# A recurrent transformer's backward chain: ScalarE's LayerNorm steps placed behind a copy, memory rows turned by TensorE, the first segment's rest rows picked by matmuls

## The chip, the cores and the metric

The kernel runs on one core of a Trainium2 chip. A core has TensorE (PE in the profile, its weight loads PEld), VectorE (DVE), ScalarE (ACT), GpSimd (POOL) and SyncE (SP); the last two also issue most of this kernel's DMAs, each engine working through its own list in order. The metric is device microseconds for one execution, as the median over runs.

## The reference

The forward is a LayerNorm, a recurrent attention over segments of 32 rows with 8 memory rows carried from one segment to the next, a second LayerNorm and a gated feed-forward layer (FFN). The kernel must return the output and the gradients of x, of the first memory and of the seven weights.

```
def _A_ref(x, mem0, Wq, Wk, Wv, Wo, seg_len):        # H=16 heads, Dh=256, M=8, D=448
    ...
    for s in range(n_seg):                            # 64 segments of 32 rows
        xs = x[:, s * seg_len:(s + 1) * seg_len, :].copy()
        h = jnp.concatenate([mem, xs], axis=1)
        q = jnp.einsum('btd,dhe->bhte', h, Wq)        # k and v alike
        ...
        scores = jnp.where(mask[None, None], scores, -1000000000.0)
        p = _softmax(scores, axis=-1)
        o = jnp.einsum('bhqk,bhke->bhqe', p, v)
        o = jnp.einsum('bhte,hed->btd', o, Wo)
        mem = o[:, :M, :].copy()
        outs.append(o[:, M:, :])
    return jnp.concatenate(outs, axis=1)
def _B_ref(x, w_gate, w_up, w_down):                  # F=1792
    return _silu(x @ w_gate) * (x @ w_up) @ w_down
h = x + _A_ref(_layernorm(x, axis=-1), A_mem0, A_Wq, A_Wk, A_Wv, A_Wo, A_seg_len)
h2 = h + _B_ref(_layernorm(h, axis=-1), B_w_gate, B_w_up, B_w_down)
# returned: h2 and the vector-Jacobian product with grad_out, x and weights in bf16
```

## The kernel before

The program has four stages: a forward chain over 64 segments, the FFN forward and backward by groups of two tiles of 128 rows, a backward chain over the segments from s = 63 down to 0, and a tail that forms the weight gradients from what the chain has stored. All loops are unrolled; a scheduler sets each engine's order from priorities and a model of the times. The block `k.prio.crit()` gives its work the highest priority. `tc.issue_after(ins)` holds what the block traces on the engine of `ins`, and on that engine alone, behind `ins` in the order; other engines' work in the block is free.

A tile t of 128 rows is four segments; r = s mod 4 counts down from 3 to 0, jm = s mod 16. In each segment TensorE forms the gradient by the output weights (L1180, evacuated to `dO_own`), turns it (L1190), multiplies for dV from the memory rows (`value_rest`, L1306, which reads `dOr` and the turned P rows `P4r`) and from the segment's own rows (`value_own`, L1312), and forms dP (L1429). VectorE makes dS from dP, from the loaded P (`P_sb`) and from its block-diagonal copy `P_bd`, which GpSimd writes (L1225). TensorE turns dS (L1475), and VectorE and ScalarE copy one half each (L75 and L76, the lines of the helper `k.evac`). The heads for dK and dQ follow (L1289), their rows are evacuated (`heads` and `first_rows`), and the rows are multiplied by the turned weights (L1324, and L1344 for the memory rows of a whole tile). The sum is taken over four partition groups (`summed`, L1330, from two ScalarE copies L1515), copied by VectorE (L1531) and turned (L1534) into the memory gradient that the next segment needs. L1531 is thus one instruction per segment, close to its end.

The LayerNorm backward of a tile runs two tiles later, inside the segments: `rest_sums_saved` stores the memory rows' sums to DXN at r = 3 (L1368), `norm_load` loads DXN, XN and DH at r = 2 (L1356 to L1359), `norm_first` is traced at the end of r = 2 and `norm_second` at the end of r = 1. Both are called in a block that holds their VectorE steps behind the last VectorE copy of `first_rows("q")`, `cast["v"]`. Their ScalarE activations are L1373 and L1384. The tile `x` of these steps appears in the profile as om; `om2`, the same buffer, also takes the memory rows' products at r = 0 (L1470).

Every 16 segments (jm = 0) the memory gradients gathered in `dmr` are turned to rows: four DMA transposes on SyncE (L1551) write `dhx`, and `memory_rows` stores it by four GpSimd DMAs (L381) to DC0 and DC1. The tile `dhx` is also the target of `prep_tile`'s DMA transpose at r = 3 (L1170) and, as `rO`, of evacuations at r = 2 and 1. The loads for the next segment on SyncE are `load_rest` (L1201, from RO), `load_p` (L1209), `load_v` (L1213) and `load_qk` (L1221); on GpSimd half of `load_p` (L1210) and P_sb (L1223).

The first segment, s = 63, is special: its memory rows' gradients are formed just ahead (b = 0, 1), stored to RO and loaded again by `load_rest(NSEG - 1)`, and its `value_rest` is placed after the scores instead of ahead of the turns:

```
            with tc.issue_after(last_d.ins):
                if s == NSEG - 1:
                    value_rest(pV)
                value_own(pV, 0 if s == NSEG - 1 else 4, 8)
```

Of the kernel before, what the change touches and what calls it, by code (L numbers as in the profile page):

```python
# [10 lines left out]
BF16 = mybir.dt.bfloat16  # L11
ALU = mybir.AluOpType
ACT = mybir.ActivationFunctionType
AX = mybir.AxisListType

P = 128
# [1116 lines left out]
def backward_chain(k: _K):  # L1133
    nc, tc = k.nc, k.tc
    S, D, M, H, Dh, HD = k.S, k.D, k.M, k.H, k.Dh, k.HD
    SEG, L, NSEG, NT, KC, DP, MC, DC = k.SEG, k.L, k.NSEG, k.NT, k.KC, k.DP, k.MC, k.DC
    ident, dr, sel = k.ident, k.dr, k.sel
    smal = k._small
    W, A, B = k.W, k.A, k.B
    OUT1, OUT2 = k.aps["out"][1][0], k.aps["out"][2][0]  # L1140
    NWIN = 8
    DQ = D // 4
# [7 lines left out]
    dmr = A(48, 4, 16, M)  # L1150
# [5 lines left out]
    do_roll = A(57.3125, 4, NWIN, L)  # L1156
    dhx = A(59.8125, 4, P)
    dOr = A(62.0625, 5, P)
# [5 lines left out]
    ot = k.identf[:, 0:DQ // 2].bitcast(BF16)  # L1164
# [22 lines left out]
    def grads_turned(bank, src, dst, b, eng="v"):  # L1187
        pt = bank[:].bitcast(BF16)
        for i in range(4):
            last = nc.tensor.transpose(pt[:, i * P:(i + 1) * P], src[:, i * P:(i + 1) * P], ident[:, :])  # L1190
        return last, k.evac(dst.rearrange("p (x c) n -> p x c n", x=2)[:, :, 8 * b:8 * b + 8, :],
                            pt[:, 0:512].rearrange("p (c x n) -> p x c n", x=2, n=32), eng)

    def rest_saved(t, b, src):
        nc.gpsimd.dma_start(out=dr["RO"][t][:, 512 * b:512 * b + 512], in_=src)

    def load_rest(s):
        t, r = divmod(s, 4)
        src = dr["RO"][t].rearrange("(q r k) n -> r q k n", q=4, k=M)
        for w, a, m, n in ((0, 0, 0, 3), (1, 0, 3, 3), (0, 3, 6, 2)):  # L1200
            nc.sync.dma_start(out=dOr[32 * w:32 * w + 32, a:a + n].rearrange("p m e -> p (m e)"), in_=src[r][:, :, P * m:P * (m + n)])  # L1201
# [49 lines left out]
    for c in range(4):  # L1251
        d0 = DQ * c
        while d0 < DQ * (c + 1):
            n = min(DQ * (c + 1), (d0 // P + 1) * P) - d0
# [13 lines left out]
    rO = dhx.rearrange("p c n -> p (c n)")  # L1268
# [3 lines left out]
    with k.prio.crit():  # L1272
        for b in range(2):
            pr, src = k.bank(b), (rO, A(46, 512))[b]
# [1 line left out]
            k.evac(src, pr[:], "vs"[b])  # L1276
            grads_turned(k.bank(2 + b), src, R4_b[(NT - 1) % 2], b, "vs"[b])
            rest_saved(NT - 1, b, src)
    load_rest(NSEG - 1)

    def c12(ps, b):
        n = min(12, 32 - 12 * b)
# [14 lines left out]
    def v_out(ps, m):  # L1297
        return v_bank(ps, m // 3)[2].rearrange("p (x m g n) -> p x m g n", x=2, g=2, n=L)[:, :, m % 3]

    def p_rows(rhs, m):  # L1300
        return rhs[:, :, m // 2].rearrange("p (x g) n -> p x g n", x=2)

    def value_rest(ps):
        for m in (0, 3, 1, 4, 2, 5, 6, 7):
            w, a = divmod(m, 3) if m < 6 else (0, m - 3)
            last = nc.tensor.matmul(v_out(ps, m), lhsT=dOr[32 * w:32 * w + 32, a, :], rhs=p_rows(P4r[32 * w:32 * w + 32], m),  # L1306
                                    start=m in (0, 3, 6), stop=False, skip_group_check=True)
        return last

    def value_own(ps, m0, m1):  # L1310
        for m in range(m0, m1):
            last = nc.tensor.matmul(v_out(ps, m), lhsT=dO_own[:, m * P:(m + 1) * P], rhs=p_rows(P4, m),  # L1312
                                    start=False, stop=True, skip_group_check=True)
        return last

    def v_rows(ps, b):
        m0, n, bank = v_bank(ps, b)
        return slice(2 * m0, 2 * m0 + 2 * n), bank.rearrange("p (x c n) -> p x c n", x=2, n=L)

    def rows_in(ps, lhs, WT, js, start=False, stop=False):  # L1320
        js = list(js)
        for i, j in enumerate(js):
            q = i % 4
            last = nc.tensor.matmul(ps[32 * q:32 * q + 32, 0:D], lhsT=lhs(j), rhs=WT[:, cj(j), :],  # L1324
                                    start=(start and i < 4), stop=(stop and i >= len(js) - 4), skip_group_check=True)
        return last
# [9 lines left out]
    def rest_parts(n):  # L1336
        last = None
        for _ in range(min(n, len(parts))):
            last = parts.pop(0)()
        return last  # L1340
# [26 lines left out]
        for q in range(4):  # L1367
            nc.gpsimd.dma_start(out=dst[q][:, 0:M], in_=pxs[32 * q:32 * q + 32])  # L1368

    def norm_first(t):  # L1370
        x, rstd, junk = norm[t][0], k.rstd1[:, t:t + 1], prod_t
        m1, m2 = [smal.tile([P, 1], FP32, name=f"lnb_m{i}") for i in (1, 2)]
        nc.scalar.activation(out=x[:], in_=x[:], func=ACT.Copy, accum_out=m1[:])  # L1373
        nc.vector.tensor_tensor_reduce(out=junk[:, 0:D], in0=x[:], in1=xn_t, scale=1.0, scalar=0.0,
                                       op0=ALU.mult, op1=ALU.add, accum_out=m2[:])
        m1s, m2s = [smal.tile([P, 1], FP32, name=f"lnb_m{i}s") for i in (1, 2)]
        nc.vector.tensor_scalar(out=m1s[:], in0=m1[:], scalar1=-1.0 / D, scalar2=rstd, op0=ALU.mult, op1=ALU.mult)
        nc.vector.tensor_scalar(out=m2s[:], in0=m2[:], scalar1=-1.0 / D, scalar2=None, op0=ALU.mult)
        nc.vector.scalar_tensor_tensor(out=x[:], in0=xn_t, scalar=m2s[:], in1=x[:], op0=ALU.mult, op1=ALU.add)
        norm[t][1] = m1s  # L1380

    def norm_second(t):
        x, m1s = norm.pop(t)
        nc.scalar.activation(out=x[:], in_=x[:], func=ACT.Identity, scale=k.rstd1[:, t:t + 1], bias=m1s[:])  # L1384
        for c0 in (0, 224):
            nc.vector.tensor_tensor(out=xn_t[:, c0:c0 + 224], in0=x[:, c0:c0 + 224], in1=dh_h[c0 // 224], op=ALU.add)
        nc.gpsimd.dma_start(out=OUT1[t * P:(t + 1) * P, :], in_=xn_t)

    V_FILL = {3: 16, 2: 16, 1: 16, 0: 3 * MC}
    for s in range(NSEG - 1, -1, -1):  # L1390
        t, r = divmod(s, 4)
        jm = s % 16
        sl = s % NWIN
# [12 lines left out]
        with k.prio.crit():  # L1406
# [6 lines left out]
            pool_op = nc.gpsimd.tensor_copy(out=doT[:, :, 0:M], in_=R4_b[t % 2][:, :, r * M:(r + 1) * M])  # L1413
# [1 line left out]
                with tc.issue_after(pool_op.ins):  # L1415
                    (rest_sums_saved if r == 3 else norm_load)(t + 2)
            pV = [k.bank(2 + b) for b in range(3)]
            if s < NSEG - 1:
                value_rest(pV)
            grads_turned(k.bank(0), dO_own[:, 0:512], doT[:, :, M:L], 0)  # L1420
            if s < NSEG - 1:
                value_own(pV, 0, 4)
            last_t, turned_v = grads_turned(k.bank(1), dO_own[:, 512:], doT[:, :, M:L], 1)

            def score_mm(hg):
# [13 lines left out]
            with tc.issue_after(last_t.ins):  # L1439
                last_d = score_mm([(1, 1), (5, 1)] + [(h, g) for h in (2, 3, 6, 7) for g in range(2)])  # L1440
            with tc.issue_after(last_d.ins):
                if s == NSEG - 1:
                    value_rest(pV)
                value_own(pV, 0 if s == NSEG - 1 else 4, 8)
            if s == 0:
                k.tl.grads(0)
                k.tl.outs(4, 7, 0, 6)
            for b in range(3):
                js, v = v_rows(pV, b)
# [10 lines left out]
            for b in range(3):  # L1460
                js, v = v_rows(pV, b)
# [11 lines left out]
            for h in range(8):  # L1473
                for g in range(2):
                    last_t = nc.tensor.matmul(pT[g][64 * g:64 * g + L, h * L:(h + 1) * L], lhsT=dS_bd[:, h, g, :],  # L1475
                                              rhs=ident[:, 64 * g:64 * g + L], start=True, stop=True, skip_group_check=True)
# [32 lines left out]
            last_r = rows_in(pH, lambda j: blk["q"][:, j, r * SEG:(r + 1) * SEG], WqT_sb, range(MC), stop=True)  # L1509
            cast = first_rows("q")  # L1510
# [7 lines left out]
            with tc.issue_after(last_r.ins):  # L1518
                if rest:
                    last_r = grads_by_col(rest_lhs, pR, 2 - r, 0, 2)  # L1520
                elif parts:
                    last_r = rest_parts(12)
            pq = k.bank(2)
            with tc.issue_after(last_r.ins):
                last_r = summed(pq, om)
            with tc.issue_after(last_r.ins):
                if rest:
                    grads_by_col(rest_lhs, pR, 2 - r, 2, 4)
                elif parts:
                    rest_parts(4)  # L1530
            nc.vector.tensor_copy(out=ot, in_=pq[:, 0:DQ])  # L1531
            if s > 0:
                pm = k.bank(3)[:].bitcast(BF16)
# [2 lines left out]
                                      in_=pm[0:DQ, 0:P].rearrange("p (c n) -> p c n", n=32)[:, :, 24:32])  # L1536
            else:
                for q in range(4):
                    nc.sync.dma_start(out=OUT2[:, DQ * q:DQ * q + DQ], in_=ot[32 * q + 24:32 * q + 32, :])
            nc.scalar.copy(out=dxs, in_=pq[:, 0:DQ])  # L1540
            if rest:
                k.evac(rO, pR[:], "s")
            if r in (2, 1) and t + 2 < NT:
                with tc.issue_after(cast["v"].ins):
                    (norm_first if r == 2 else norm_second)(t + 2)
        pool_op = nc.gpsimd.tensor_copy(out=dmr[0:DQ, :, jm, :], in_=do_roll[0:DQ, :, sl, SEG:L])
        stores("start", s, pool_op.ins)
        if jm == 0:
            rows = dhx.rearrange("p c n -> p (c n)")
            for c in range(4):  # L1550
                nc.sync.dma_start_transpose(out=rows[:, DQ * c:DQ * c + DQ], in_=dmr[0:DQ, c].rearrange("p s m -> p (s m)"))  # L1551
            k.tl.memory_rows(s // 16, rows)
        if s % 4 == 1 and 16 <= s < 48:
            with tc.issue_after(pool_op.ins):
# [20 lines left out]
    for t in (1, 0):  # L1575
        if t == 0:
            rest_parts(len(parts))
            nc.scalar.copy(out=om2[:], in_=pX[:, 0:D])
            rest_out()
        rest_sums_saved(t)  # L1580
        norm_load(t)
        norm_first(t)
        norm_second(t)
    assert not pending


# [243 lines left out]
```

## Time and profile before

| | |
|---|---|
| runs before, median (lowest, highest of 3) | 2954.59 us (2947.98, 2963.27) |
| profiled execution, its time | 2945.84 us |
| profiled execution, span of its instructions | 2943.8 us |
| mean granted TensorE clock | 0.980 |
| TensorE busy (matmul) | 2742.8 us, 93% |
| DVE, ACT, POOL busy | 1303.8, 1046.0, 930.3 us |
| backward chain, first to last L1531 | 1299.71 to 2258.21 us |

The page of the profile gives busy times, the span in slices, DMA queues, the chain of work that ended last, and the costliest groups of instructions. In timeline rows the columns are the start (us from the span's start), the duration in us, the engine, line, operation, the tiles written and read, the count, and in brackets the engine's idle time before the row with what ended it. "PEclk" and "granted clock" are the share of full speed that TensorE was given. A row of the waits gives who waited for whom, the total in us, how many times, and the longest. SPq and POOLq rows are DMA issues and other sequencer work.

### The profile page before, as it was taken

What the parts mean: (1) busy time and instruction counts of PE and PEld (TensorE: products, weight loads), DVE (VectorE), ACT (ScalarE), POOL (GpSimd) and SP (SyncE); (2) the same over time, 40 slices, a digit from 0 to 9 for tenths busy, and PEclk for the clock granted to TensorE, in tenths of its full rate; (3) what the DMA queues carried; (4) which work ended last, traced back from release to release, by engine and by line L of the source; (5) the groups of instructions that cost most, each with busy time, mean ns of one, the idle gap of its engine ahead of it and who ended that gap; (6) DMA issues with size and microseconds to landing.
All of it is one profiled execution on the core that took longest, in us unless ns stands there. A gap on an engine that the chain in (4) does not pass through costs nothing.

```text
span 2943.8 us, 97992 instructions
## 1 busy us (share of the span) xinstructions
PE 2742.8 (93%) x41631; PEld 1579.9 (54%) x41631; DVE 1303.8 (44%) x3351; ACT 1046.0 (36%) x2574; POOL 930.3 (32%) x2063
## 2 busy tenths in 40 slices
PE   4999999999999999979899998999998999999999
PEld 3555565566555556645555555555554444444444
DVE  4555555565555666734545554554543011111110
ACT  2555455454445444423333333333332010111210
POOL 1222232232232222424544445444453111112211
PEclk9999999999999999989999999999999999999999
DMA  7577777677678989976766667676677998969951
GB/s 256 154 191 192 194 193 195 187 196 200 196 192 238 273 216 215 244 229 161 173 162 174 167 161 181 168 178 167 161 169 201 351 261 183 171 190 229 190 158 53
DMA packets 784281, 572.06 MB, mean 194 GB/s; under 512 B 634748, under 2 KB 676100, under 8 KB 781284
## 3 DMA queue, kind: packets, MB, share of 16 engines
q1 hardware_dynamic: 719636, 407.84, 58.5%
q0 software_dynamic: 64208, 157.95, 17.1%
q8 instruction: 328, 5.37, 0.8%
q14 instruction: 109, 0.89, 0.1%
HBM read 181.64 MB, written 244.92 MB: 145 GB/s over the span
## 4 chain that ended last, share of the span: by engine, by line
PE 66%; DMA 10%; issue 9%; DVE 4%; POOL 4%; ACT 4%; SPq 1%; POOLq 0%; ACTq 0%; DVEq 0%
PE psf L1671 8%; PE bank L1324 6%; PE psf L590 6%; PE psf L725 5%; PE psf L988 4%; PE po L772 4%; PE bank L1180 4%; PE fx L1112 3%; PE fx L1671 3%; PE psf L614 2%; DMA arB<-P_all 2%; PE bank L1289 2%; PE bank L1344 2%; PE psf L506 1%; DMA DXN<-arA 1%
## 5 line engine op out<-in xcount | busy, mean ns | idle before, releaser
L75 DVE CAST arA<-psf 128x512 bf16<-128x512 f32 (+2 forms) x285 | 160.0, 562 | 491.9 <-PE psf L1671 249.9
L76 ACT CAST arA<-psf 128x512 bf16<-128x512 f32 (+3 forms) x379 | 190.0, 510 | 528.7 <-PE psf L1671 215.1
L1324 PE MATMUL bank<-arW,arA 128*32 128x448 bf16 x6144 | 327.6, 364 | 0.0
L76 ACT CAST arA<-bank 128x384 bf16<-128x384 f32 (+4 forms) x607 | 193.1, 376 | 113.7 <-PE bank L1312 98.6
L1671 PEld LDWEIGHTS <-arA 128*128 128x128 bf16 x1440 | 139.6, 99 | 162.4 <-issue 7.9
L1324 PEld LDWEIGHTS <-arA 128*32 128x32 bf16 x6144 | 158.2, 99 | 125.6 <-issue 13.1
L1671 PE MATMUL psf<-arW,arA 128*128 128x512 bf16 x882 | 224.6, 383 | 0.0
L725 PE MATMUL psf<-arW,arA 128*64 128x512 bf16 x1536 | 212.2, 382 | 0.0
L590 PE MATMUL psf<-arW,arA 128*32 128x512 bf16 x3072 | 189.8, 381 | 7.7 <-DVE arA L75 0.9
L988 PE MATMUL psf<-arW 128*128 128x256 bf16 (+1 forms) x1288 | 148.0, 276 | 5.6 <-DVE arA L75 4.3
L75 DVE CAST arA<-bank 128x384 bf16<-128x384 f32 (+4 forms) x385 | 130.4, 392 | 51.6 <-PE bank L1289 48.2
L1225 POOL COPY arB<-arB 40x320 bf16<-40x320 bf16 x128 | 68.0, 532 | 231.5 <-DMA arB<-P_all 193.1
L1748 POOL DMA_DIRECT2D out_dram<-arA x96 | 52.1, 544 | 263.6 <-DVE arA L75 236.9
L1210 POOL DMA_DIRECT2D arA<-P_all x256 | 128.0, 504 | 21.2 <-issue 20.4
L988 PEld LDWEIGHTS <-arW 128*128 128x128 bf16 (+1 forms) x1344 | 103.0, 97 | 56.9 <-issue 45.7
L1289 PE MATMUL bank<-arB,arW 128*128 128x80 bf16 x2048 | 96.2, 204 | 38.2 <-ACT arB L76 35.7
L1180 PE MATMUL bank<-arW,arA 112*32 112x512 bf16 x2048 | 129.0, 396 | 1.3 <-DVE arA L1535 1.3
L772 PE MATMUL po<-arW,arA 128*32 128x256 bf16 (+1 forms) x4096 | 126.9, 261 | 1.2 <-DVE arA L75 1.2
L590 PEld LDWEIGHTS <-arA 128*32 128x32 bf16 x3072 | 70.3, 96 | 105.1 <-issue 28.5
L1711 PE MATMUL psf<-arW 128*128 128x448 bf16 x525 | 114.5, 360 | 2.7 <-ACT arA L76 2.7
L772 PEld LDWEIGHTS <-arA 128*32 128x32 bf16 x4096 | 104.0, 96 | 8.5 <-DVE arA L75 1.5
L1289 PEld LDWEIGHTS <-arW 128*128 128x128 bf16 x2048 | 83.4, 101 | 45.3 <-issue 37.1
(311 smaller groups left out, 5050.5 us busy)
## 6 DMA issues: line engine op xcount, KB each, us to landing
arW<-T SPq DMA_DIRECT2D x256, 128.0 KB
X_o<-arA SPq DMA_DIRECT2D x37, 512.0 KB
T<-arA SPq DMA_DIRECT2D x64, 256.0 KB
X_v<-arA POOLq DMA_DIRECT2D x30, 512.0 KB, 4.6
X_k<-arA POOLq DMA_DIRECT2D x30, 512.0 KB, 3.9
X_q<-arA POOLq DMA_DIRECT2D x30, 512.0 KB, 4.7
out_dram<-arA POOLq DMA_DIRECT2D x84, 128.0 KB, 5.0
VG<-arA SPq DMA_DIRECT2D x64, 160.0 KB
```

The source lines that it names most:

```text
L75: return nc.vector.tensor_copy(out=out, in_=in_)
L76: return nc.scalar.copy(out=out, in_=in_)
L590: nc.tensor.matmul(banks[b][w][32 * q:32 * q + 32, :], lhsT=hT_roll[:, kc, sl, M:L], rhs=(Wq_sb, Wk_sb)[w][:, kc, col(q, b)], start=(b == ...
L725: nc.tensor.matmul(pV[b][64 * g:64 * g + 64, 0:512], lhsT=hT_flat[:, kc, sl * L:sl * L + 64], rhs=Wv_sb[:, kc, n * 512:(n + 1) * 512], sta ...
L772: last = nc.tensor.matmul(pO[32 * q:32 * q + 32, 0:w], lhsT=xblk[:, j, r * SEG:(r + 1) * SEG], rhs=Wo_sb[:, cj(j), 256 * dh:256 * dh + w], ...
L988: nc.tensor.matmul(ps[fp][:, f2 * 256:(f2 + 1) * 256], lhsT=Wt[lo:hi, kc, c * P:(c + 1) * P], rhs=xT[lo:hi, kc, :], start=(kc == 0 and f2 ...
L1180: last = nc.tensor.matmul(bank[32 * q:32 * q + 32, :], lhsT=lhs(c), rhs=WoT_sb[0:DQ, c, n0:n0 + 512], start=(c == 0), stop=(c == 3), skip_ ...
L1210: nc.gpsimd.dma_start(out=P4[32 * q:32 * q + 32, 2 * x + g], in_=pa[64 * g + M:64 * g + L, x])
L1289: last = nc.tensor.matmul(ps[b][:, i * 2 * L:(i + 1) * 2 * L], lhsT=lhs[:, at, :], rhs=rhs_bd[:, cl // 2, :, :].rearrange("p g n -> p (g n ...
L1324: last = nc.tensor.matmul(ps[32 * q:32 * q + 32, 0:D], lhsT=lhs(j), rhs=WT[:, cj(j), :], start=(start and i < 4), stop=(stop and i >= len( ...
L1671: k.last_mm = nc.tensor.matmul(pa[i][:, 0:w], lhsT=lhs_of(b)[:, i // 2 * P:(i // 2 + 1) * P], rhs=rhs_of(q, b, i % 2), start=(b == 0), sto ...
L1711: k.last_mm = nc.tensor.matmul(pa[i][:, 0:D], lhsT=lhs_of(b, i), rhs=rhs_of(b), start=(bi == 0), stop=(bi == m + 3))
```

## The change

Three edits in `backward_chain`. First, the activations of `norm_first` and `norm_second` are held on ScalarE behind `cast["s"]`, the ScalarE copy of `first_rows("q")` of the segment in which they are traced. Second, at jm = 0 the four DMA transposes are replaced by four TensorE transposes into bank 4, behind the last `summed` matmul, and a ScalarE copy into `dhx`; the GpSimd copy into `dmr` that feeds them is traced earlier and inside the high-priority block, in all segments. Third, `load_rest(NSEG - 1)` is replaced: GpSimd copies 32 columns of the identity into `one`, four matmuls with it pick the rows of r = 3 from the two halves still in SBUF, and two copies write `dOr`; `value_rest` and `value_own` of s = 63 stand where they do in all other segments.

```diff
-    load_rest(NSEG - 1)
+        one = ot[:, 0:32]
+        nc.gpsimd.tensor_copy(out=one.rearrange("p (q m) -> p q m", m=M), in_=ident[:, :].rearrange("p (q r m) -> p r q m", q=4, m=M)[:, 3])
+        half = A(46, 512)
+        pk = [k.bank(2), k.bank(3)]
+        for out, src in ((pk[0][0:32, 0:384], rO[:, 0:384]), (pk[0][32:64, 0:P], rO[:, 384:512]),
+                         (pk[0][32:64, P:384], half[:, 0:256]), (pk[1][0:32, 0:256], half[:, 256:512])):
+            nc.tensor.matmul(out, lhsT=one, rhs=src, start=True, stop=True, skip_group_check=True)
+        k.evac(dOr[0:64, 0:3].rearrange("p m e -> p (m e)"), pk[0][0:64, 0:384], "v")
+        k.evac(dOr[0:32, 3:5].rearrange("p m e -> p (m e)"), pk[1][0:32, 0:256], "s")
...
-    def norm_first(t):
+    def norm_first(t, after):
...
-        nc.scalar.activation(out=x[:], in_=x[:], func=ACT.Copy, accum_out=m1[:])
+        with tc.issue_after(after["s"].ins):
+            nc.scalar.activation(out=x[:], in_=x[:], func=ACT.Copy, accum_out=m1[:])
...
-    def norm_second(t):
+    def norm_second(t, after):
         x, m1s = norm.pop(t)
-        nc.scalar.activation(out=x[:], in_=x[:], func=ACT.Identity, scale=k.rstd1[:, t:t + 1], bias=m1s[:])
+        with tc.issue_after(after["s"].ins):
+            nc.scalar.activation(out=x[:], in_=x[:], func=ACT.Identity, scale=k.rstd1[:, t:t + 1], bias=m1s[:])
...
-            if s < NSEG - 1:
-                value_rest(pV)
+            value_rest(pV)
             grads_turned(k.bank(0), dO_own[:, 0:512], doT[:, :, M:L], 0)
-            if s < NSEG - 1:
-                value_own(pV, 0, 4)
+            value_own(pV, 0, 4)
...
             with tc.issue_after(last_d.ins):
-                if s == NSEG - 1:
-                    value_rest(pV)
-                value_own(pV, 0 if s == NSEG - 1 else 4, 8)
+                value_own(pV, 4, 8)
...
+            pool_op = nc.gpsimd.tensor_copy(out=dmr[0:DQ, :, jm, :], in_=do_roll[0:DQ, :, sl, SEG:L])
+            if jm == 0:
+                with tc.issue_after(last_r.ins):
+                    pr = k.bank(4)[:].bitcast(BF16)
+                    for c in range(4):
+                        nc.tensor.transpose(pr[:, DQ * c:DQ * c + DQ], dmr[0:DQ, c].rearrange("p s m -> p (s m)"), ident[0:DQ, 0:DQ])
             nc.vector.tensor_copy(out=ot, in_=pq[:, 0:DQ])
...
             nc.scalar.copy(out=dxs, in_=pq[:, 0:DQ])
+            if jm == 0:
+                rows = dhx.rearrange("p c n -> p (c n)")
+                k.evac(rows[:, 0:D], pr[:, 0:D], "s")
             if rest:
                 k.evac(rO, pR[:], "s")
             if r in (2, 1) and t + 2 < NT:
                 with tc.issue_after(cast["v"].ins):
-                    (norm_first if r == 2 else norm_second)(t + 2)
-        pool_op = nc.gpsimd.tensor_copy(out=dmr[0:DQ, :, jm, :], in_=do_roll[0:DQ, :, sl, SEG:L])
+                    (norm_first if r == 2 else norm_second)(t + 2, cast)
         stores("start", s, pool_op.ins)
         if jm == 0:
-            rows = dhx.rearrange("p c n -> p (c n)")
-            for c in range(4):
-                nc.sync.dma_start_transpose(out=rows[:, DQ * c:DQ * c + DQ], in_=dmr[0:DQ, c].rearrange("p s m -> p (s m)"))
             k.tl.memory_rows(s // 16, rows)
```

The two calls for the last tiles, after the loop, pass `cast` in the same way.

More of the change, by code (lines that the diff above doesn't have):

```diff
@@ L1581, in backward_chain @@
         norm_load(t)
-        norm_first(t)
-        norm_second(t)
+        norm_first(t, cast)
+        norm_second(t, cast)
     assert not pending
```

## The prediction

> **What bounds the kernel now.** I read the page first: TensorE is busy for 93% of the span, so only stretches in which it stands still, or runs below full clock, have time to give.
>
> ```profile
> span 2943.8 us, 97992 instructions
> PE 2742.8 (93%) x41631; PEld 1579.9 (54%) x41631; DVE 1303.8 (44%) x3351; ACT 1046.0 (36%) x2574; POOL 930.3 (32%) x2063
> ```
>
> The backward chain's length per segment can be read from the DVE rows of L1531, one at the end of each segment. The first comes at 1299.71, the last at 2258.21. With r = s mod 4, segments with r = 2 last 13.98 us, with r = 1 14.09, with r = 0 14.4 to 15.0 (medians or extremes of 15 or 16). With r = 3 they last 15.2 to 21.4, except s = 59, the only one without a LayerNorm step in flight: 13.84. So the loss sits in r = 3. The windows view, cut at the L1531 rows, for s = 51, 43, 35 and 59 (columns: window, length, busy PE, PEld, DVE, ACT, POOL, granted clock, DMA share, GB/s):
>
> ```profile
> 1456.87:1478.22 21.35, 16.03 (x275) 9.13 (x273) 7.13 (x18) 5.40 (x17) 10.86 (x22) 0.84 0.87 171
> 1583.70:1601.11 17.41, 15.31 (x275) 8.76 (x273) 7.04 (x18) 5.40 (x17) 11.39 (x25) 0.90 0.75 191
> 1704.62:1721.10 16.48, 13.62 (x275) 8.19 (x273) 7.04 (x19) 5.40 (x17) 9.60 (x19) 1.00 0.95 200
> 1341.32:1355.16 13.84, 13.62 (x275) 8.12 (x273) 6.95 (x19) 4.73 (x15) 7.75 (x19) 1.00 0.75 163
> ```
>
> The same matmuls (x275) take 13.62 us warm and up to 16.03 after a stall: a stall costs its idle time and then slow matmuls. Who stalls is in the timeline of s = 51:
>
> ```profile
> 1466.86 0.54 POOL L1356 DMA_DIRECT2D om<-DXN  x1 [3.90 <-DMA DXN<-arA]
> 1469.70 0.58 ACT L1373 ACTIVATE om<-om 128x448 f32<-128x448 f32 x1 [6.43 <-DMA om<-DXN]
> 1470.87 1.23 PE L1289 MATMUL bank<-arB,arW 128*128 128x80 bf16 x16 [5.14 <-ACT arB L76]
> 1472.02 5.06 PE L1324 MATMUL bank<-arW,arA 128*32 128x448 bf16 x64
> 1477.45 0.96 POOL L1225 COPY arB<-arB 40x320 bf16<-40x320 bf16 x2 [5.93 <-DMA arB<-P_all]
> ```
>
> ScalarE waits at norm_first's activation (L1373) for a load; behind it in ScalarE's order stands the second half of dS turned (L76), and TensorE's heads (L1289) wait for that. The waits of ScalarE between 1390 and 2245 us say how often, and the next two fences show the change's other two places: SyncE's transposes at s = 48 with the matmul that the loads behind them hold up, and the first segment.
>
> ```profile
> ACT om L1373 <- DMA om<-DXN: 54.9, 14, 6.5
> ```
>
> ```profile
> 1511.12 6.70 SPq L1551 DMA_TRANSPOSE arA<-arA  x4
> ...
> 1523.57 0.41 PE L1306 MATMUL bank<-arA 32*128 32x160 bf16 x2 [2.74 <-DMA arA<-P_all]
> ```
>
> ```profile
> 1286.85 0.58 PE L1306 MATMUL bank<-arA 32*128 32x160 bf16 x3 [11.48 <-DMA arA<-RO]
> 1280.00:1285.00 5.00, 0.00 (x0) 0.00 (x0) 0.00 (x0) 0.00 (x0) 0.00 (x0) 0.50 1.01 417
> 1290.00:1295.00 5.00, 5.00 (x61) 2.72 (x59) 0.81 (x2) 1.85 (x8) 2.18 (x5) 0.51 0.11 24
> ```
>
> **Part 1, the LayerNorm activations.** In the program text norm_first belongs to r = 2, but only its DVE steps are held there; L1373 ran 17 to 19 us ahead of them (1407.96 against 1424.95, 1469.70 against 1488.92), in r = 3, as soon as its load was thought to be there. Pinned behind the ScalarE copy of first_rows at the end of r = 2, it cannot stand in r = 3. The 14 segments with r = 3 that carry it (s = 55 to 3) sum to 261.8 us; 14 x 13.84 is 193.8; the excess is 68.0. Eleven of them (all but s = 47, 31, 15) have 199.3 - 152.2 = 47.1 of it. That is the gross gain.
>
> What is late next: POOL. It stops at L1356 until DXN has landed, and the loads of P for the next segment queue behind it. In the trace the copy L1225, which starts when P has landed, comes 13.6 to 21.6 us after the r = 3 segment began. The next segment reads P 5.04 us after its start, so with 13.84 long segments it is needed at 18.9. Three of the eleven rows are past it (20.6, 21.3, 21.6: 1.7 + 2.4 + 2.7 = 6.8 us). The ends are 0 and all fourteen as late as the worst, 38. The DMA engines were busy for 0.75 to 0.95 of the ordinary r = 3 segments, and the same transfers must now go through less time, so I take 12: nearer the three rows than the worst. Net 35.1.
>
> At its new place L1373 costs nothing by its cover: in r = 2 ScalarE is free from 1424.24 to 1426.65 and needs 0.58 + 0.19 us. DVE's L1374 to L1379 wait for it and end near 1426.7; L1531, queued behind them on DVE, ran at 1428.38. If that cover were gone it would cost up to the 1.7 us of these DVE steps each time. norm_second's L1384 (0.76 us) moves from the end of r = 2, where the copy L1515 stood behind it (TensorE idle 0.40 before L1330), to the end of r = 1, where ScalarE idles 2.68 us before L1515. The r = 2 segments without it last 13.74 (s = 58) against 13.98: 0.24 x 14 = 3.4 gained; ends 0 and 14 x 0.40 = 5.6.
>
> The slow matmuls: PE busy in these 14 segments sums to 211.4 us, 20.7 over 14 x 13.62; so 20.7 of the 68.0 are slower matmuls, at a granted clock of 0.83 to 0.92, and 47.3 idle time. The Trainium skill ("TensorE: Matmul & The Clock Gate", Part 1, What's actually happening) has the array drop to half clock only after an idle window of about 3.4 us. By that rule the 9.7 us of slow matmuls in s = 47, 43, 39, 27 and 19, whose longest gaps were 2.74, 1.97, 2.76, 3.18 and 3.07 us, would have another cause and stay. The trace speaks against it: the clock was 0.90 in s = 43 after a gap of 1.97 and 1.00 where nothing stalled, so the sum counts them as returned.
>
> **Part 2, memory rows.** At s = 48, 32, 16 and 0 the four DMA transposes go, 6.70 us of SyncE's queue at s = 48; the loads for s = 47 follow them at once. Four TensorE transposes come (four of L1190 take 0.40 us) and one ScalarE copy of 128x448 from PSUM (0.59 for 128x512); TensorE may pay 0.25 to 0.4 a time before L1534: 1.0 us in all. The copy is covered by ScalarE's 2 us gap after L1540; bank 4, which it empties, is next written by L1306's last three, some 2.7 us later. The three segments after, s = 47, 31 and 15, have 20.9 us of the excess, 10.9 of it TensorE idle at L1306. But the tile they leave, dhx, takes the next DMA transpose of a block on SyncE (L1170), which waits for POOL's four DC stores to land: it came 10.0 us into s = 47 against 3.2 in s = 51, and the loads for s = 46 stand behind it, ending 16.5 in. With 14 us segments that is late by 2 to 3 us. I return half: 10.5; ends 2 and 20.9.
>
> **Part 3, the first segment.** The round trip through DRAM (store 11.59 us, load 10.04, in the chain of waits) goes; one POOL copy, four matmuls of under 0.4 us and two copies of some 0.5 come, 1 to 1.5 us on the path, before value_rest. TensorE stood still 11.48 + 0.75 us. But until some 1287 us the DMA engines are full (share 1.01, 417 GB/s, then 0.11): the last weights, Tq, issued to 1268.2, would land only then, and this segment's last L1324 rows need them. So the segment can end about 1289 to 1291 instead of 1299.71: 9.5. Ends: 4, if the rest rows for s = 62, still loaded from DRAM behind those weights, stall the next; 18, if the weights are there in time and it lasts some 14.5 us.
>
> **The tail** begins with SyncE's four transposes (4.98 us) ahead of its loads and stores, and TensorE waits 2.67 us at 2297.53 for a copy whose buffer waits on POOL's stores behind them: 2, ends 0 and 4.4.
>
> **Sum:** 35.1 + 3.4 + 10.5 - 1.0 + 9.5 + 2.0 = 59.5. The profiled execution took 2945.84 us (span 2943.8): 2886.3. The median of the runs is 2954.59, 8.75 above it: 2895.
>
> **Rivals.**
>
> *POOL's chain becomes the wait* (DXN landed, norm loads, P): all 14 tiles 2.7 late, 38, and half of them with a slow stretch of 1.6, 11. Gain 59.5 + 12 - 49 = 22.5: 2932. For it: POOL is busiest in r = 3, with the DMA share at 0.95; against: eight of eleven rows have room. 0.10.
>
> *Only the pins pay*, since the weights and dhx hold the other two: 35.1 + 3.4 - 1.0 = 37.5: 2917. 0.10.
>
> *The slow stretches do not go with the stalls*: 59.5 - 9.7 = 49.8 gained, 2905. 0.05. The clock gate rule above is what would make it so.
>
> *No change:* the pin orders L1373 but something else holds L1289 in r = 3; 2951. s = 59 speaks against it. 0.04.
>
> *Slower:* DVE now waits at L1374 for L1373 with L1531 behind, one for one, if the load of om lands later than the end of r = 2, about 24 us after r = 3 began, plus 1.7 of room. To end 15 us above today each of 14 tiles must lose (59.5 + 15) / 14 = 5.3, a landing at 31: 2970. The trace has it at 12.8 in s = 51 and, at the latest, at 15.0 in s = 31. 0.03.
>
> My forecast keeps 0.68, its own range 2866 to 2922: the ends of Parts 2 and 3 and of the return, not all at once. The range for 8 in 10 takes in the second and third rival as well and part of the first: 2866 to 2928. A measurement of this kernel can tell about 0.5%, 14.8 us. Faster by more: 0.68 + 0.10 + 0.10 + 0.05 = 0.93; within: 0.04; slower: 0.03.
>
> **What would show it.** In the changed profile: L1373's successor waits for no load within the loop (54.9 us before); r = 3 lasts 14 to 16 at clock 1.00; no gap before L1289 above 1 us; L1306 in the first segment waits under 2 us and L1324 there waits for weights until 1287; L1551's transposes are gone. Segments with r = 2 that grow to 15 or more, with DVE or POOL waiting for P_all, would show the return larger than 12. I am wrong if r = 3 stays above 16, or the first L1531 row stays past 1297.

## The result, and the profile after

The changed kernel takes 2915.52 us (median of 4 runs, 2906.24 to 2923.81) against 2956.34 before: a ratio of 0.9862, 95% interval 0.9823 to 0.9902. Run again later beside other kernels it took 2900.41 (6 runs, 2884.97 to 2914.42) against 2966.79, a ratio of 0.978 (0.9739 to 0.982). So it is faster by 1.4 to 2.2%; the two intervals just miss each other, and the first is the one that the forecast of 2895 us (2866 to 2928) was made for. 2915.52 lies inside that range. The profiled execution took 2906.24 us, 39.6 less than the 2945.84 before; 59.5 were forecast. In the changed file L1531 is L1543, L1373 L1382, L1289 L1297, L1306 L1314, L1312 L1320 and L1324 L1332.

The page first. TensorE is as busy as before, in a shorter span:

```profile
span 2904.4 us, 98035 instructions
PE 2741.1 (94%) x41647; PEld 1580.4 (54%) x41651; DVE 1307.8 (45%) x3352; ACT 1047.0 (36%) x2579; POOL 925.3 (32%) x2064
```

Second, the waits of TensorE inside the backward chain. Before, 1305 to 2245 us (who waited for whom; total, times, longest):

```profile
PE bank L1289 <- ACT arB L76: 35.7, 13, 5.2
PE bank L1306 <- DMA arA<-P_all: 11.2, 4, 4.4
PE bank L1330 <- ACT om L1515: 4.4, 14, 0.5
```

After, 1305 to 2215 us:

```profile
PE bank L1314 <- DMA arA<-P_all: 13.8, 5, 4.7
PE bank L1320 <- DMA arA<-P_all: 12.6, 6, 4.4
```

The heads' wait for ScalarE is gone, and of the 14 short ones behind norm_second one is left (L1338, 0.5 us). ScalarE's L1382 no longer waits for the load of om anywhere in the loop; the two such waits that are left, 25.3 us, are of the last two tiles, behind the loop. In their place stand waits for P, six of them at a line that had none: L1320, `value_own`.

Third, the windows view, cut at the end-of-segment rows. Before, s = 50 (s = 51 and 43 of before stand in the prediction):

```profile
1478.22:1492.20 13.98, 13.59 (x273) 8.11 (x273) 8.36 (x24) 5.37 (x16) 7.33 (x17) 1.00 0.49 133
```

After, s = 51, 50 and 43:

```profile
1456.00:1469.74 13.74, 13.60 (x275) 8.12 (x273) 6.95 (x19) 4.73 (x15) 9.87 (x20) 1.00 0.88 191
1469.74:1488.65 18.91, 16.42 (x273) 9.51 (x273) 8.60 (x23) 5.29 (x17) 7.37 (x19) 0.82 0.76 168
1579.71:1593.45 13.74, 13.60 (x275) 8.12 (x273) 6.94 (x18) 4.73 (x15) 9.97 (x20) 1.00 0.82 183
```

s = 51 fell from 21.35 to 13.74 us with TensorE at full clock, and the segment after it, s = 50, rose from 13.98 to 18.91. The same over the whole chain, summed in us from the end-of-segment rows (L1531 before, L1543 after). "Ordinary" are the eleven tiles other than those of s = 47, 31 and 15:

| | before | after | after, second execution |
|---|---|---|---|
| end of s = 63 (from the last FFN matmul L1112) | 42.4 | 35.0 | 34.1 |
| s = 62 | 13.6 | 18.6 | 16.1 |
| r = 3, eleven ordinary | 199.3 | 155.8 | 154.0 |
| r = 3, s = 47, 31, 15 | 62.5 | 41.2 | 41.3 |
| r = 2, eleven ordinary | 154.1 | 171.7 | 167.0 |
| r = 2, s = 46, 30, 14 | 42.3 | 59.3 | 60.4 |
| from the last L1543 to the end | 685.6 | 678.5 | 686.9 |

All r = 3 segments together gave 64.8 us; the r = 2 segments behind them took 34.6 back.

The wait of s = 50 in the timeline:

```profile
1465.36 0.54 POOL L1364 DMA_DIRECT2D om<-DXN  x1 [3.25 <-DMA DXN<-arA]
1467.48 1.98 POOL L1210 DMA_DIRECT2D arA<-P_all  x4
1475.65 0.69 PE L1320 MATMUL bank<-arA,om 128*128 128x160 bf16 x4 [2.46 <-DMA arA<-P_all]
```

POOL stands 3.25 us for DXN, then issues the LayerNorm loads, then the four P4 loads. The last two of these, 10 KB each, landed 6.4 and 6.5 us after their issue, at 18.8 and 19.5 us after s = 51 began; `value_own` of s = 50 would have read them at 17.0 (3.3 us into a segment that does not stall).

The wait of s = 46 goes through SyncE:

```profile
1522.34 2.36 POOL L381 DMA_DIRECT2D DC<-arA  x4
1526.58 1.22 SPq L1170 DMA_TRANSPOSE arA<-DHb  x1
1527.89 2.03 SPq L1201 DMA_DIRECT2D arA<-RO  x3
1529.97 4.54 SPq L1209 DMA_DIRECT2D arA<-P_all  x8
1535.71 0.42 PE L1314 MATMUL bank<-arA 32*128 32x160 bf16 x2 [4.68 <-DMA arA<-P_all]
```

The block transpose L1170 into dhx comes 9.4 us into s = 47, after SyncE has waited 6.1 us for the DC stores (L381) to land, and the loads for s = 46 stand behind it.

The first segment, in the waits of TensorE from 1262 to 1300 us, and its successor in the windows view:

```profile
PE bank L1332 <- DMA arW<-Tq: 4.7, 2, 3.5
PE bank L1332 <- DMA arW<-Tv: 2.1, 1, 2.1
```

```profile
1290.00:1295.00 5.00, 3.92 (x40) 1.34 (x37) 0.56 (x3) 0.85 (x3) 0.99 (x5) 0.50 0.59 126
1295.00:1300.00 5.00, 5.00 (x50) 2.67 (x42) 1.43 (x3) 1.21 (x3) 0.00 (x0) 0.50 0.43 92
1300.00:1305.00 5.00, 5.00 (x79) 2.65 (x79) 2.43 (x5) 1.12 (x5) 2.94 (x6) 0.56 0.15 34
1305.00:1310.00 5.00, 4.98 (x107) 2.98 (x103) 2.53 (x9) 2.14 (x7) 0.90 (x2) 1.00 0.71 186
```

The wait for the rest rows became a wait for weights, as forecast. But s = 62, which begins at 1291.92, then ran at half clock for its first 12 us or so, with TensorE busy nearly throughout.

### The profile page after: what moved, and what is told of

The parts are those of the page before. It is cut to its first block, busy times and chain, and to the rows that moved or that the text cites. A ratio compares the mean times of both kernels' runs of the same rounds, so it can differ in the third digit from the quotient of the medians.

```text
span 2904.4 us, 98035 instructions
## 1 busy us (share of the span) xinstructions
PE 2741.1 (94%) x41647; PEld 1580.4 (54%) x41651; DVE 1307.8 (45%) x3352; ACT 1047.0 (36%) x2579; POOL 925.3 (32%) x2064
## 4 chain that ended last, share of the span: by engine, by line
PE 68%; DMA 12%; issue 8%; POOL 4%; ACT 3%; DVE 3%; SPq 1%; POOLq 0%; ACTq 0%; DVEq 0%
PE psf L1682 8%; PE bank L1332 7%; PE psf L590 6%; PE psf L725 5%; PE po L772 4%; PE bank L1180 4%; PE psf L988 4%; PE fx L1682 3%; PE fx L1112 3%; PE psf L614 2%; PE bank L1297 2%; DMA arA<-P_all 2%; PE psf L506 2%; DMA arB<-P_all 2%; PE bank L1437 1%
## 5 line engine op out<-in xcount | busy, mean ns | idle before, releaser
L1332 PE MATMUL bank<-arW,arA 128*32 128x448 bf16 x6144 | 322.4, 359 | 6.9 <-DMA arW<-Tq 4.7
L76 ACT CAST arA<-bank 128x96 bf16<-128x96 f32 (+4 forms) x608 | 193.5, 376 | 121.8 <-PE bank L1320 102.9
L1332 PEld LDWEIGHTS <-arA 128*32 128x32 bf16 x6144 | 156.3, 97 | 128.3 <-issue 14.3
L75 DVE CAST arA<-bank 128x256 bf16<-128x256 f32 (+4 forms) x386 | 129.4, 390 | 9.5 <-PE bank L1297 4.2
L76 ACT CAST arB<-psf 128x64 bf16<-128x64 f32 (+1 forms) x192 | 65.1, 341 | 97.9 <-PE psf L597 75.6
L1297 PE MATMUL bank<-arB,arW 128*128 128x80 bf16 x2048 | 94.7, 202 | 4.1 <-issue 2.4
```

Of the source, the lines that this page charges most:

```text
L75: return nc.vector.tensor_copy(out=out, in_=in_)
L76: return nc.scalar.copy(out=out, in_=in_)
L1297: last = nc.tensor.matmul(ps[b][:, i * 2 * L:(i + 1) * 2 * L], lhsT=lhs[:, at, :], rhs=rhs_bd[:, cl // 2, :, :].rearrange("p g n -> p (g n ...
```

## The experiments

**Each part alone, on the kernel before.** One profiled execution each; the kernel before took 2957.08 us beside them. `e1_pins` has the `issue_after(after["s"].ins)` of `norm_first` and `norm_second`; `e2_rows` the four TensorE transposes, their copy and the moved `pool_op`; `e3_first` the picks, with `value_rest` and `value_own` of s = 63 in their usual places.

> Part 1 alone on the kernel before: the two activations pinned, nothing else. Theory (stalls in r = 3 were ScalarE's, and POOL's P loads are what is late next): the eleven ordinary r = 3 segments fall to 13.7 to 15.2 us as in the changed kernel (sum 156 instead of 199); the ordinary r = 2 segments rise to a sum of about 172 instead of 154, waiting for P4; s = 47, 31 and 15 keep their wait at the P4r loads and stay at 18 to 20, and s = 46, 30, 14 stay at 14. First segment and tail as before. About 30 us gained, profiled time 2916. Rival (the pins do little without the other two parts): under 15 us, r = 3 stays above 16.

> Part 2 alone on the kernel before: memory rows turned by TensorE. Theory (the block transpose into dhx waits for the DC stores): s = 47, 31 and 15 lose their wait at P4r but keep ScalarE's, 16 to 19 us instead of 20.5 to 21.2; s = 46, 30, 14 rise by 0 to 3 each; the tail, without four transposes ahead of SyncE's loads, gains 4 to 7 between the last segment and the end. Profiled time 2933 to 2940. Rival (the tail's gain has another source): tail as before, 2940 to 2946.

> Part 3 alone on the kernel before: rest rows of the first segment picked by matmuls. Theory (the weights Tq and a slow clock take the gain back): first end-of-segment row near 1292 instead of 1299.7, and s = 62 at about 18.5 us instead of 13.6 with the granted clock at 0.5 for most of it; net 2 to 4 us, profiled time about 2943. Rival (s = 62 was slow for another part of the change): s = 62 stays near 14 and 7 to 8 us are gained.

| us | e1_pins | e2_rows | e3_first |
|---|---|---|---|
| profiled time | 2908.95 | 2946.29 | 2967.55 |
| end of s = 63 from L1112 | 42.2 | 41.5 | 34.3 |
| s = 62 | 13.6 | 13.6 | 18.7 |
| r = 3, eleven ordinary / s = 47, 31, 15 | 152.1 / 60.5 | 208.2 / 56.4 | 205.2 / 64.1 |
| r = 2, eleven ordinary / s = 46, 30, 14 | 158.2 / 41.4 | 154.3 / 42.2 | 154.0 / 41.9 |
| last end-of-segment row to the end | 691.4 | 679.6 | 698.5 |

The pins did what was expected of them in r = 3, and 2908.95 is about as good as the whole change, because the ordinary r = 2 segments, expected at 172 in sum, rose by 4 us only, not by 18. Part 2 alone took 6 us from s = 47, 31 and 15 and 6 from the tail, as expected, while the eleven ordinary r = 3 segments took 8.9 us more than before (208.2 against 199.3; with e3_first's 205.2 that is the spread of three executions without the pins, and its cause is open). The time was 10.8 us below the kernel before beside it and missed the 2933 to 2940 expected. s = 46, 30 and 14 did not rise, neither here (42.2) nor with the pins alone (41.4): only where both are in do they return 17 us. Part 3 alone missed its time: in its own place it did what was expected, 8 us gained in s = 63 and 5 lost in s = 62, but the rest of that execution was longer, in the tail above all. There TensorE waited 17.7 and 8.2 us for VectorE (L1656, the copies of packed memory blocks), places that vary in all executions here: the first of these waits was 7.3 us in the profile before, 5.6 and 20.3 in two executions of the changed kernel. A single time can't judge a part of 3 us in this kernel; the segments can.

**Where the pins' gain goes: the order on POOL.** In the changed kernel, the LayerNorm loads are held behind the next segment's P loads and P_bd copy.

```diff
+        k.pbd_op = pool_op                      # in load_qk, after the two P_bd copies
         stores("mid", s, pool_op.ins)
...
-                with tc.issue_after(pool_op.ins):
+                with tc.issue_after((pool_op if r == 3 else k.pbd_op).ins):
                     (rest_sums_saved if r == 3 else norm_load)(t + 2)
```

> The changed kernel, with the four LayerNorm loads on POOL held behind the P loads and the P_bd copy of the next segment, instead of ahead of them. Theory A (the order on POOL's queue is what made P4 late in r = 2): the ordinary r = 2 segments return from a sum of 171.7 us to 152 to 157, s = 46, 30, 14 stay near 20; 15 to 19 us gained on the changed kernel, profiled time 2887 to 2892. Theory B (in 14 us the DMA engines cannot move what r = 3 asks for, in any order): the ordinary r = 2 segments keep over half of their 20 us of excess or hand it to r = 1, profiled time 2897 or more.

It took 2876.4 us (one execution). The ordinary r = 2 segments came back to 152.5 us, as theory A has it; s = 46, 30 and 14 kept 62.1. No wait at `value_own` (here L1321) is left in the list of TensorE's waits between 1305 and 2200 us, whose first line is now

```profile
PE bank L1315 <- DMA arA<-P_all: 15.3, 6, 5.1
```

and its timeline at s = 51 shows P ahead of the LayerNorm loads:

```profile
1457.81 2.06 POOL L1210 DMA_DIRECT2D arA<-P_all  x4
1459.86 0.56 POOL L1223 DMA_DIRECT2D arB<-P_all  x1
1463.88 0.55 POOL L1365 DMA_DIRECT2D om<-DXN  x1
```

POOL no longer stops for DXN before these loads, and the second P4 load landed 2.5 us after its issue. So theory A stands for the place of the wait: order, not too many bytes. The gain on the changed kernel, 30 us in these two executions where 15 to 19 were expected, holds 10 us of the tail, which is not to be counted.

**The rows' buffer.** On top of that, the rows go to xn_t, which is free at that time.

```diff
-                rows = dhx.rearrange("p c n -> p (c n)")
+                rows = xn_t if s > 0 else dhx.rearrange("p c n -> p (c n)")
                 k.evac(rows[:, 0:D], pr[:, 0:D], "s")
```

> The kernel with late norm loads, and in it the memory rows written to xn_t instead of dhx for s > 0, so that the block transpose L1170 on SyncE no longer waits for the four DC stores. Theory A (dhx is what holds SyncE's loads for s = 46, 30, 14): these three fall from a sum of 62.1 us to 41 to 43, and nothing else moves; 19 to 21 us gained on that kernel, profiled time near 2856. Theory B (the DC stores and the stores beside them fill the DMA engines, whatever the buffer): the three stay at 55 or more.

s = 46, 30 and 14 fell from 62.1 to 42.1 us, s = 46 to 13.74. L1170, 9.4 us into s = 47 in the changed kernel, now came 2.4 us in (the segment begins at 1507.93):

```profile
1510.32 1.21 SPq L1170 DMA_TRANSPOSE arA<-DHb  x1
```

The waits for P in the chain are down to 1.3 us:

```profile
PE bank L1315 <- DMA arA<-P_all: 1.3, 2, 0.8
```

Timed, it took 2866.71 us (6 runs, 2862.27 to 2877.73) against 2966.79: a ratio of 0.9672 (0.9633 to 0.9712), and the changed kernel 2900.41 beside it. This is the version that beats both. The profiled time, 2867.71 us, missed the 2856 expected: of the 20.0 us gained on e4_late_norm_loads in these three segments, s = 62 took back 2.8 (18.63 against 15.85), s = 0 2.2 and the tail 5.8.

**The clock in s = 62.** 24 matmuls that nobody reads fill TensorE's wait for Tq.

```diff
+            if s == NSEG - 1:
+                with tc.issue_after(last_kr.ins):       # last_kr: the last row matmul of dK
+                    for i in range(24):
+                        last_f = nc.tensor.matmul(pX[:, 0:D], lhsT=ident[:, :], rhs=WvT_sb[:, i, :], start=True, stop=True, skip_group_check=True)
+            with tc.issue_after(last_f.ins) if s == NSEG - 1 else nullcontext():
                 last_r = rows_in(pH, lambda j: blk["q"][:, j, r * SEG:(r + 1) * SEG], WqT_sb, range(MC), stop=True)
```

> The kernel with late norm loads and rows in xn_t, and in the first segment 24 added matmuls of 448 columns whose result nobody reads, between the rows of dK and the rows of dQ, where TensorE waits for the weights Tq. Theory A (s = 62 is long because the clock falls to half in that wait and stays there): with the filler s = 62 lasts 13.7 to 14.3 us, and the first segment ends at most 1 to 2 us later. Theory B (s = 62 is long because its own loads are late): s = 62 keeps 15.8 us or more.

> The kernel with late norm loads, rows in xn_t and the filler, timed. If the slow clock in s = 62 is worth the 3.8 us that the single look showed (18.6 to 14.8), it is 2 to 6 us under the kernel without the filler (2866.71 us median, ratio 0.9672): ratio 0.964 to 0.967. If the clock would have recovered elsewhere anyway, the ratio stays within 0.001 of 0.9672. s = 62 again at 14 to 15 us.

s = 62 without the filler (e5_rows_xn) and with it, in the windows view:

```profile
1292.90:1311.53 18.63, 18.02 (x255) 9.63 (x257) 6.95 (x18) 4.73 (x15) 4.07 (x9) 0.66 0.50 120
```

```profile
1287.17:1301.97 14.80, 13.13 (x255) 7.70 (x257) 6.95 (x18) 4.73 (x15) 4.07 (x9) 1.00 0.51 127
```

The same 255 matmuls took 13.13 us instead of 18.02, and the clock was full: theory A, though 14.80 is above the 14.3 expected, since 1.67 us of idle time remained. The first segment did not end later (33.3 us after L1112, 34.5 without). Both executions with the filler had 14.8. In the times it can't be seen: 2864.38 us (6 runs) against 2955.51 is a ratio of 0.9693 (0.9665 to 0.9722), above the 0.9672 without, each measured against its own runs of before. The expected 0.964 to 0.967 was missed, and so was the 0.9672 within 0.001 of the other case; what 3.8 us are worth in the median stays open.

**The same kernels again, and the pins with the late loads.**

> The changed kernel once more, unaltered, beside the others on the same chip. Theory A (P4 is late in r = 2 by the order on POOL, the same in every execution): the ordinary r = 2 segments again sum to 168 to 175 us. Theory B (P4 lands within 2 us of when it is needed, and small differences in the DMA timing decide which segments stall): the sum differs from 171.7 by more than 6 us, and other segments stall. s = 46, 30, 14 again near 20 each under both. Time within 2900 to 2925.

> The pins alone once more, unaltered. Theory A (parts 2 and 3 cost the ordinary r = 2 segments some 13 us): they again sum to 155 to 160 us. Theory B (chance in the DMA timing): the sum is above 163 or below 154, and other segments stall than s = 10 and 26. s = 47, 31, 15 again at 19 to 21 each.

> The pins alone, timed beside the others. Theory A (parts 2 and 3 return nearly all that they gain: the DC stores move the stall of s = 47, 31, 15 to s = 46, 30, 14, and the slow clock in s = 62 takes back most of the first segment): a ratio to the kernel before within 0.006 of the changed kernel's, 0.978 to 0.986, and s = 47, 31, 15 again at 59 to 62 us in sum. Theory B (they are worth their share): 0.990 or more.

> The pins and the late norm loads on the kernel before, without parts 2 and 3. The ordinary r = 2 segments stay at 151 to 154 us in sum and the ordinary r = 3 at 152 to 155; s = 47, 31, 15 at 59 to 62 and the first segment as before, s = 62 at 13.6. Time some 8 us under the pins alone, ratio 0.972 to 0.980. If the order of the loads on POOL were not the cause of the waits at P4, ordinary r = 2 segments of 17 us and more would be left.

The ordinary r = 2 segments summed to 171.7 and 167.0 us in two executions of the changed kernel, and to 158.2, 162.8 and 170.0 in three of the pins alone. Which segments stall changes too: s = 54, 50, 38, 22, 10 and 2 at L1320 in the first execution, 34, 10 and 2 in the second. Both numbers of the second executions, 167.0 and 162.8, fell between the bounds of their two theories. So which segments stall differs from execution to execution, at the place that the order on POOL makes (chance in the DMA timing would do that, but was not isolated); whether parts 2 and 3 add to it, as the lower sums of two of three executions with pins alone suggest, is not settled. With the late loads on the pins alone the sum was 152.4, as with the whole change (152.5, 151.7, and 152.3 and 153.0 with the filler): four different kernels with that order, none with a wait at `value_own`.

Timed, the pins alone took 2911.07 us, a ratio of 0.9837 (0.9806 to 0.9868), between the two measurements of the changed kernel (0.9862, 0.978). So no worth of parts 2 and 3 shows in the time of the changed kernel. They pay once their own returns are taken away: pins and late loads have 0.9797 (0.9769 to 0.9826), 14.1 us under the pins alone where some 8 were expected, with s = 47, 31 and 15 still at 61.7 us; with parts 2 and 3, the free buffer and the filler, timed beside them, it is 0.9693.

## Why the prediction was right or wrong

The time fell inside the range, but the profiled gain is 19.9 us short of the sum, and the misses point one way: the return took 8.2 us more than forecast, part 2 brought 6.2 less and part 3 6.7 less, the stalls in r = 3 3.6 less. The range was drawn for these ends "not all at once"; they came nearly all at once, and a tail that gave 5.1 us too much made up for a part.

**The stall in r = 3** was read rightly: a load that ScalarE waited for, the heads behind it. 47.1 us were put on the eleven ordinary segments, 43.5 and 45.3 came. The slow matmuls went with the stalls: PE busy fell from 16.03 to 13.60 us in s = 51 and from 15.31 to 13.60 in s = 43, one of the five segments in which a rival had them stay; that rival fell. The Trainium skill ("TensorE: Matmul & The Clock Gate", Part 1, What's actually happening) has the clock fall only after an idle window of some 3.4 us; here s = 50 ran at 0.82 after a gap of 2.46 us, so trace and rule differ again.

**The return** was mis-sized: 12 us, with the order on POOL named as the cause, and all fourteen tiles late, 38 us, as the far end. The ordinary r = 2 segments rose 17.6 us over before, and the forecast, with the 0.24 saved in each, had them rise 9.4. Its price went by when P_sb is read (18.9 us after r = 3 began); what came late first was P4, on the same queue and read 1.8 us earlier, and TensorE's slow stretch after each stall was left out of the sum. The rival in which POOL's chain becomes the wait had counted it and put 49 us on all r = 2 segments; they rose 34.6. Of these, 17.6 are its mechanism, the order on POOL, which e4_late_norm_loads took away; the other 17.0, in s = 46, 30 and 14, stayed in that run (62.1 us) and went only with the other buffer for the rows: they came by dhx and SyncE's queue.

**Part 2** had the right mechanism, dhx and the DC stores, and too low a price. Of 21.3 us gained in s = 47, 31 and 15, 17.0 went back in s = 46, 30 and 14: 4.3, where half, 10.5, was forecast. A lateness of 2 to 3 us was counted; the gaps were 4.7, 3.8 and 2.7, and each was followed by a clock of about 0.83 over the segment. The 1.0 us for the TensorE transposes did not show at s = 48, 32 and 16 (14.40, 14.40 and 14.98, as before); s = 0 grew by 1.1, and the transposes behind its end-of-segment row waited 2.9 us for the copy into dmr, a wait that counts with the tail.

**Part 3** failed in its last step. The first segment ended at 1291.92, near the 1289 to 1291 forecast, held by Tq as said. But the forecast ended the sum there and took the next segment at its usual length: 5.0 of the 7.8 us went into s = 62 at half clock. Net 2.8, under the lower end of 4.

**norm_second's** 3.4 us can be read where r = 2 does not stall: 13.74 in s = 34 and 26, against 13.98.

**The tail** gave 7.1 in the profiled execution for 2. The wait of 2.67 us that was named is gone, and the one of 2.9 us for the copy into dmr has come. What gave the gain are TensorE's waits for the copies of packed memory blocks. Before and after, behind the last end-of-segment row:

```profile
PE ph L1652 <- DVE arW L75: 18.4, 3, 7.3
```

```profile
PE ph L1663 <- DVE arW L75: 9.8, 2, 5.6
```

These fell by 8.6 us, more than the whole gain. The prediction has no such term, so as far as this wait goes its tail was right in sign by luck. Over all profiled executions the tail took 668.4 to 679.6 us in six of the seven with part 2 and 686.9 in the seventh, against 685.0 to 698.5 in the six without it (means 677.8 and 688.9). So part 2 seems to shorten it by more than the 2 us; why these copies come earlier stays open.

For the whole chain, the last end-of-segment row came at 2225.95 instead of 2258.21 us, 32.3 earlier, against 57.5 forecast without the tail.

## What to carry to other kernels

A wait that is removed should be followed through the list of every in-order queue that it had been hiding: give each load its landing and the time at which it is read in the shortened stage, and take the first reader, not the best known one. Place loads with much slack behind those that are read next, above all when the first of them waits for a store. A buffer shared by two uses carries a wait from one queue into another, and a segment's gain should be read together with the next two segments'.

## What the runs showed of the hardware that was not expected

TensorE stayed at half clock from 1290 to about 1304 us in the changed kernel, though it was busy for 13.9 of the 15 us from 1290 to 1305; earlier in the same execution it had come back within 4 us (granted clock 0.55, 0.50, 0.50, 0.74 and 1.00 in the five microseconds from 1277 to 1282, TensorE busy for 4.86 of them). In three more kernels s = 62 behaved like this (18.7, 18.6 us) or in part (15.9), and in the kernels without part 3 it never did (13.6). The Trainium skill ("TensorE: Matmul & The Clock Gate", Part 1, What's actually happening) has one busy window of some 3.4 us restore the clock; the rows from 1277 agree, those from 1290 do not. 24 matmuls of 128x128 weights in the wait ahead of s = 62 kept the clock at 1.00; why the segment's own matmuls did not bring it back was not tried.

A 10 KB load issued by POOL took 6.4 us to land behind four LayerNorm loads of 112 to 224 KB, and 2.5 us ahead of them.
